# A convolution's prologue reordered: x ahead of the diagonal, its first rows on SP's queue, bands summed on TensorE, exchanged weights on VectorE and GpSimd

## The chip, the cores and the metric

The kernel runs on one core of one Trainium2 chip. The time is the device time of one execution in microseconds; the kernel before took 530.68 us (median of 3 runs, 530.61 to 530.69). The engines are named as in the profile: PE is TensorE (PEld its weight loads), DVE is VectorE, ACT is ScalarE, POOL is GpSimd, SP is SyncE, which here only issues transfers. PSUM is the memory that PE writes; SBUF is the working memory.

## What is computed

A causal convolution with 7 taps along the sequence, one set of taps (a softmax of 7 weights) for each of 8 heads of 24 channels, and behind it a feed-forward network of two products multiplied with each other, and two more products:

```python
w = exp(weight - max); w = w / sum(w)                 # (8 heads, 7 taps)
out[b, s, h, :] = sum_k w[h, k] * x_pad[b, s + k, h, :]   # x_pad: 6 zero rows ahead
x = out.reshape(31232, 192)
a = x @ w1; b = x @ w2                                # 192 -> 1024
h = a * b @ w3                                        # 1024 -> 1024
return h @ w_out                                      # 1024 -> 192
```

x is 8 x 3904 x 192 in float32. The products run in bfloat16; w3 and w_out are multiplied with each other once, so that the last two products become one.

## The kernel before

**Two streams.** The 31232 tokens are cut into two streams (NS = 2, index r) of 15616 tokens, which share every matmul's place on the array: stream r uses rows 64 r to 64 r + 63, where a third of the 192 channels lies (NP = 3 thirds, index k). Tokens are worked in rounds R of 512 per stream (CH). For each round, `first_product` makes 8 feature tiles (index ft) of 128 features: `pa` = x w1 and `pb` = x w2, each of 6 matmuls (3 thirds, 2 streams); ACT copies pa to SBUF (`asb`, line 366) and DVE multiplies it with pb into `abT` (line 367). `second_product` multiplies abT with W_sb = w3 w_out and stores the result.

**Exchanged weights.** Since stream 1 sits on the other 64 rows, half of the weights are needed with their two halves of 64 rows exchanged. `wn[0..2]` hold w1 and w2 as loaded (wn[0] w1's first 128 rows, wn[1] those of w2, wn[2] the last 64 of both); `wsw[0..2]` hold the exchanged copies (`ws` in the profile), which `swap_w(k, lo, hi, engines)` makes for a range of columns with two copies of 64 rows. pa uses wn[0], wsw[0], wn[2] and wsw[2]; pb uses wn[1], wsw[1], wn[2] and wsw[2]. Feature tile ft uses columns 128 ft to 128 ft + 127.

**Convolution.** x is loaded as windows of 32 rows (C), 26 outputs each (ST = C - 6), in batches b of 20 to 80 windows. For each head a band matrix `Aband` of 32x32 carries the taps, so that a window times the band is the convolution (`conv`, line 252, 32x32 places on the array). The band is the same in all four groups of 32 partitions. The result goes by ACT or DVE from PSUM to `convo` (line 260), is transposed (by PE for the first batches, `first_transposes` for batch 0, lines 309 to 321) into `xT`, and feeds `first_product`. `load_x` (lines 105 to 134) issues the transfers of a batch, one for each stream r for batches 0 to 2, all on POOL's queue, with a cast from float32 to bfloat16. The very first window of each stream needs zeros ahead, so it is left out of the runs: DVE zeroes its slot (line 114) and `load_first` (lines 137 to 141) fetches its 26 rows by two more transfers on POOL's queue.

**The bands before.** Line 146 to 150: POOL fills `diag` with ones and selects its diagonal. DVE builds `cmask` for all 7 taps, four copies with a sliding window (lines 162 to 167). The softmax runs on the taps (lines 191 to 199, DVE, ACT, DVE, DVE) into `share`; one matmul (line 201) spreads it over 128 partitions; DVE casts it into `wsb` (line 204), multiplies mask and weights for 8 heads, 7 taps and 32 columns into `cprod` (line 211), and sums the taps by three additions (lines 217 to 220) into Aband.

**What sets the order.** Each engine executes its instructions in the order in which the program lists them (the schedule is manual). POOL's list is: diagonal, batch 0 of x, its first rows, 8 weight transfers in two halves of columns (`load_w`), batches 1 and 2 of x, six exchange copies of the second half of the columns (line 339, 64x512), w_out and four blocks of w3. A transfer on POOL's queue is issued there and its bytes then come in behind those issued before. `warm(n)` puts n matmuls on zeros into PE's list (line 187): 6 at the start, 8 after the spreading, 2 after batch 0's convolution. Four PSUM tiles of two banks ("banks") are used in turn for everything.

The exchange copies of columns 0 to 511 are made by DVE and ACT, the first 256 around `first_transposes` (lines 435 to 437), the second 256 after feature tile 0 (line 459). The convolution of batch 1 follows feature tiles 4 and 5, that of batch 2 feature tile 7 and the next round's 0.

Of the kernel before, what the change touches and what calls it, by code (L numbers as in the profile page):

```python
# [16 lines left out]
def kernel(  # L17
# [84 lines left out]
                runs.append([s, tok(i), 1])  # L102
        return runs

    def load_x(b, parts=(0, 1)):
        tiles = xb_of.setdefault(b, {})
        zeros_of = zero_rows.setdefault(b, [])
        n, m, E = shape_of(b)
        for js in [v for q, v in enumerate(parts_of(b)) if q in parts]:
            xb = work.tile([128, len(js) * m, D], BF16, tag="xb", bufs=6, name="xb")  # L110
            for j in js:
                tiles[j] = (xb, (j - js[0]) * m)
            if b == 0:
                nc.vector.memset(xb[:, 0, :], 0.0)
            for e in range(E):
                for s, t, w in runs_of(b, js, e):
                    for r in range(NS):
                        nc.gpsimd.dma_start(  # L118
                            out=xb[group(r, e), s:s + w, :],
                            in_=bass.AP(tensor=x.tensor, offset=(r * TS + t - PAD) * D,  # L120
                                        ap=[[D, C], [E * ST * D, w], [1, D]]))
# [13 lines left out]


    def load_first():
        xb = xb_of[0][0][0]
        for r in range(NS):
            nc.gpsimd.dma_start(out=xb[Q * r + PAD:Q * r + C, 0, :],  # L140
                                in_=x_rows[r * TS:r * TS + ST, :])
# [6 lines left out]
    nc.gpsimd.affine_select(  # L148
        out=diag, in_=diag, pattern=[[-1, 128 + K - 1]], compare_op=ALU.is_equal,
        fill=0.0, base=0, channel_multiplier=1)  # L150
    ident = diag[:, 0:128]
    zeros = const.tile([128, CH], BF16)
    nc.vector.memset(zeros, 0.0)  # L153
# [6 lines left out]
    one_rows = const.tile([H, 128], BF16)  # L160
    nc.vector.memset(one_rows, 1.0)
    cmask = const.tile([128, K, C], BF16)
    for i in range(4):
        d = diag[i * C:i * C + C, i * C:i * C + C]
        nc.vector.tensor_copy(
            out=cmask[i * C:i * C + C],
            in_=bass.AP(tensor=d.tensor, offset=d.offset, ap=[d.ap[0], [1, K], [1, C]]))
# [16 lines left out]
    def warm(n):  # L184
        t = banks("warm")
        for j in range(n):
# [3 lines left out]

    low = const.tile([H, 1], FP32)
    total = const.tile([H, 1], FP32)
    share = const.tile([H, H, K], BF16)
# [3 lines left out]
    nc.vector.scalar_tensor_tensor(  # L197
        out=share, in0=taps.unsqueeze(1).to_broadcast([H, H, K]), scalar=total,
        in1=diag[0:H, 0:H].unsqueeze(2).to_broadcast([H, H, K]), op0=ALU.mult, op1=ALU.mult)
# [3 lines left out]
    wsb = const.tile([128, H, K, 2], BF16)  # L203
    nc.vector.tensor_copy(
        out=wsb, in_=spread[:, 0, 0:H * K].rearrange("p (h k) -> p h k", h=H)
            .unsqueeze(3).to_broadcast([128, H, K, 2]))
    warm(8)

    Aband = const.tile([128, H, C], BF16)
    cprod = stage.tile([128, H, K, C], BF16, tag="cprod", bufs=1, name="cprod")  # L210
    nc.vector.tensor_tensor(
        out=cprod.rearrange("p h k (s two) -> p h k s two", two=2),
        in0=cmask.rearrange("p k (s two) -> p k s two", two=2).unsqueeze(1)
            .to_broadcast([128, H, K, C // 2, 2]),
        in1=wsb.unsqueeze(3).to_broadcast([128, H, K, C // 2, 2]),
        op=ALU.mult)
    for o, i0, i1 in ((cprod[:, :, 0:3], cprod[:, :, 0:3], cprod[:, :, 4:7]),
                      (cprod[:, :, 0:2], cprod[:, :, 0:2], cprod[:, :, 2:4]),
                      (Aband, cprod[:, :, 0], cprod[:, :, 1])):
        nc.vector.tensor_tensor(out=o, in0=i0, in1=i1, op=ALU.add)  # L220


    xT = [const.tile([128, RING], BF16, name=f"xT{k}", tag=f"xT{k}") for k in range(NP)]
# [85 lines left out]
    def first_transposes(between):  # L309
        n = SIZES[0] // 4  # L310
        convo = convo_of[0]
        for k, f in enumerate((nc.scalar.copy, nc.vector.tensor_copy, nc.vector.tensor_copy)):
            tps = banks_bf16("tps")
            for w in range(n):
                nc.tensor.transpose(  # L315
                    out=tps[:, w, :],
                    in_=convo[:, w, k].rearrange("p r g -> p (r g)"), identity=ident)
            if k == 1:
                between()
            f(out=xT[k][:, 0:4 * n * ST].rearrange("p (c w s) -> p c w s", c=4, w=n),  # L320
              in_=tps[:, 0:n, :].rearrange("p w (c s) -> p c w s", c=4)[:, :, :, 0:ST])

# [75 lines left out]
    def load_wo():  # L398
        nc.gpsimd.dma_start(out=wo_b, in_=wor)
# [51 lines left out]
    def later_loads():  # L451
# [103 lines left out]
```

## Time and profile before

| | us |
|---|---|
| median of 3 runs | 530.68 |
| the profiled execution | 530.6 |
| its span, first to last instruction | 528.9 |
| PE busy | 520.7 (98%) |
| first convolution matmul (line 252) | 7.33 |
| first matmul of the first product (line 360) | 9.90 |
| first multiplication into abT (line 367) | 12.27 |
| convolution of batch 1 | 17.79 |

All times in a view of the profile count from the span's start. The page gives busy times, 40 equal slices of the span, and groups of instructions; the chain of waits goes back from the last instruction to what released it; a timeline lists instructions of an engine in order, merged where the same follow each other (start, length, engine, line, operation, tile, shapes, count, and in brackets the idle time before and what ended it). "Issue" of a transfer is the instruction on the engine whose queue it is; "landing" is when its semaphore is raised.

### The profile page before, as it was taken

The numbers are of one execution on the slowest core, as the hardware profiler recorded it, in microseconds if no ns is written. First come the engines' busy times: TensorE is split into PE (matmuls) and PEld (weight loads), VectorE is DVE, ScalarE is ACT, GpSimd is POOL, SyncE is SP. The second block draws the span as 40 slices with busy tenths as digits, with TensorE's granted clock in tenths as the row PEclk, the third lists the DMA queues.
The fourth block names the chain that finished last, engine by engine and source line by source line (L and its number), as shares of the span: only waits on it lengthen the run. The fifth ranks groups of instructions, "written<-read, shape, count | busy, mean of one in ns | idle before, by whom it ended". The sixth has DMA issues, their size and how long they took to land.

```text
span 528.9 us, 14824 instructions
## 1 busy us (share of the span) xinstructions
PE 520.7 (98%) x6461; PEld 337.8 (64%) x6462; DVE 343.2 (65%) x328; ACT 335.1 (63%) x391; POOL 67.6 (13%) x123
## 2 busy tenths in 40 slices
PE   8999999999999999999999999999999999999997
PEld 3455674856758466584765847558475575856777
DVE  6776549578394774938659295692957839377370
ACT  4867557576574766747667475765757657475562
POOL 9745002004020010301002020020000000000000
PEclk9999999999999999999999999999999999999999
DMA  9999969966699476994769946795317543130304
GB/s 115 182 198 186 141 145 149 148 157 76 145 149 170 97 93 134 128 186 92 106 137 134 178 90 102 143 163 130 56 60 144 101 134 84 62 104 9 113 2 150
DMA packets 135321, 64.69 MB, mean 122 GB/s; under 512 B 88150, under 2 KB 134232, under 8 KB 135256
## 3 DMA queue, kind: packets, MB, share of 16 engines
q1 hardware_dynamic: 92264, 45.63, 41.1%
q0 software_dynamic: 42976, 18.11, 31.8%
q8 instruction: 50, 0.82, 0.6%
q14 instruction: 15, 0.12, 0.1%
q10 hardware_dynamic: 16, 0.00, 0.0%
HBM read 36.22 MB, written 34.80 MB: 134 GB/s over the span
## 4 chain that ended last, share of the span: by engine, by line
PE 94%; DVE 2%; ACT 2%; DMA 1%; issue 1%; POOL 0%; ACTq 0%; POOLq 0%
PE ops L378 31%; PE pa L360 29%; PE pb L360 29%; PE cps L252 3%; DVE abT L367 2%; ACT asb L366 1%; PE wps L418 1%; DMA xb<-in_x_dram 1%; PE w3ps L409 1%; ACT convo L260 0%; POOL xb L118 0%; PE tps L315 0%; DVE xT L307 0%; ACT osb L383 0%; DVE xT L320 0%
## 5 line engine op out<-in xcount | busy, mean ns | idle before, releaser
L367 DVE TENSOR_TENSOR abT<-asb,pb 128x1024 bf16<-128x1024 bf16 (+1 forms) x248 | 298.2, 1204 | 89.9 <-ACT asb L366 72.7
L366 ACT CAST asb<-pa 128x1024 bf16<-128x1024 f32 (+1 forms) x248 | 247.8, 999 | 64.4 <-PE pa L360 63.6
L360 PE MATMUL pb<-xT,wn 64*128 64x512 bf16 (+1 forms) x744 | 199.2, 373 | 0.4
L360 PE MATMUL pa<-xT,wn 64*128 64x512 bf16 (+1 forms) x744 | 198.5, 373 | 0.7 <-DVE xT L307 0.5
L360 PE MATMUL pa<-xT,ws 64*128 64x512 bf16 (+1 forms) x744 | 198.6, 373 | 0.5 <-DVE ws L339 0.4
L360 PE MATMUL pb<-xT,ws 64*128 64x512 bf16 (+1 forms) x744 | 196.5, 373 | 0.0
L360 PEld LDWEIGHTS <-wn 64*128 64x128 bf16 x1488 | 137.3, 94 | 85.1 <-issue 3.5
L360 PEld LDWEIGHTS <-ws 64*128 64x128 bf16 x1488 | 129.8, 94 | 73.2 <-issue 3.4
L378 PE MATMUL ops<-W_sb,abT 128*128 128x192 bf16 x1952 | 168.2, 246 | 0.0
L378 PEld LDWEIGHTS <-abT 128*128 128x128 bf16 x1952 | 159.0, 98 | 9.3 <-issue 9.0
L383 ACT COPY osb<-ops 128x768 f32<-128x768 f32 (+1 forms) x62 | 48.9, 788 | 110.7 <-PE ops L378 110.7
L260 DVE CAST convo<-cps 128x320 bf16<-128x320 f32 (+4 forms) x44 | 31.6, 749 | 76.1 <-PE cps L252 76.1
L118 POOL DMA_DIRECT2D xb<-in_x_dram x74 | 48.4, 663 | 13.0 <-DMA xb<-in_x_dram 5.5
L260 ACT CAST convo<-cps 128x640 bf16<-128x640 f32 (+4 forms) x60 | 34.7, 625 | 5.5 <-PE cps L252 5.3
L510 POOL COPY pace<-abT 1x2 bf16<-1x2 bf16 x9 | 1.6, 174 | 252.9 <-DVE abT L367 252.9
L252 PE MATMUL cps<-xb,Aband 32*32 32x240 bf16 (+2 forms) x1344 | 16.8, 238 | 1.0 <-DMA xb<-in_x_dram 0.8
L252 PEld LDWEIGHTS <-Aband 32*32 32x32 bf16 x1344 | 9.8, 88 | 9.2 <-issue 7.3
L418 PE MATMUL wps<-wo_b,w3T 128*128 128x192 bf16 x64 | 6.6, 246 | 0.2 <-DVE xT L307 0.2
L187 PE MATMUL warm<-zeros 128*128 128x512 bf16 x15 | 5.6, 523 | 1.3 <-DVE zeros L153 1.3
L409 PEld LDWEIGHTS <-w3b 128*128 128x128 bf16 x64 | 3.7, 97 | 3.4 <-issue 3.4
L420 ACT CAST W_sb<-wps 128x192 bf16<-128x192 f32 x8 | 2.5, 318 | 5.1 <-PE wps L418 5.1
L418 PEld LDWEIGHTS <-w3T 128*128 128x128 bf16 x64 | 5.2, 98 | 0.8 <-DVE w3T L412 0.4
(49 smaller groups left out, 51.7 us busy)
## 6 DMA issues: line engine op xcount, KB each, us to landing
out_dram<-osb SPq DMA_DIRECT2D x60, 384.0 KB
xb<-in_x_dram POOLq DMA_DIRECT2D x44, 240.0 KB, 7.7
rows<-convo SPq DMA_DIRECT2D x18, 240.0 KB
rows<-convo SPq DMA_DIRECT2D x18, 150.0 KB
w3b<-in_moe_w_dram POOLq DMA_DIRECT2D x8, 256.0 KB, 9.1
xb<-in_x_dram POOLq DMA_DIRECT2D x6, 228.0 KB, 4.4
xT<-rows SPq DMA_TRANSPOSE x84
rows<-convo SPq DMA_DIRECT2D x11, 120.0 KB
```

Source lines behind the costliest of these rows:

```text
L118: nc.gpsimd.dma_start(out=xb[group(r, e), s:s + w, :], in_=bass.AP(tensor=x.tensor, offset=(r * TS + t - PAD) * D, ap=[[D, C], [E * ST * D ...
L187: nc.tensor.matmul(t[:, j % 2, :], zeros[:, 0:128], zeros, start=True, stop=True)
L252: nc.tensor.matmul(o.rearrange("p (w g) -> p w g", g=wd)[:, :, q * G:(q + 1) * G], Aband[group(r, e), h0 + q, :], xb[group(r, e), s:s + m, ...
L260: f(out=convo[:, e::E, k, :, c0:c0 + c] .rearrange("p w r g -> p r w g"), in_=src[:, :, :, o:o + c])
L360: nc.tensor.matmul(p[:, r, 0:N], w_of(i, k, r)[rs, ft * 128:(ft + 1) * 128], xT[k][rs, r0:r0 + N], start=(k == 0), stop=(k == NP - 1))
L366: nc.scalar.copy(out=asb[:, :, 0:N], in_=pa[:, :, 0:N])
L367: nc.vector.tensor_tensor(out=ab[:, ft, :, 0:N], in0=asb[:, :, 0:N], in1=pb[:, :, 0:N], op=ALU.mult)
L378: nc.tensor.matmul(ops[:, g // 2, (g % 2) * D:(g % 2) * D + D], ab[:, jt, r, g * 128:(g + 1) * 128], W_sb[:, jt, :], start=(jt == 0), stop ...
L383: nc.scalar.copy(out=osb.rearrange("p (a g) d -> p a (g d)", g=2), in_=ops[:, 0:ng // 2, 0:2 * D])
L409: nc.tensor.transpose(out=tps[:, gt, :], in_=w3b[:, gt * 128:(gt + 1) * 128], identity=ident)
L418: nc.tensor.matmul(wps[:, 0, 0:D], w3T[:, gt, :], wo_b[:, gt, :], start=(gt == 0), stop=(gt == JT - 1))
L420: nc.scalar.copy(out=W_sb[:, jt, :], in_=wps[:, 0, 0:D])
```

## The change

It touches only the prologue and the order of the lists.

- **x.** `load_x` takes a list of streams and keeps its tile between calls. Stream 0 of batch 0 is issued as POOL's first instruction, ahead of the diagonal; stream 1 behind the diagonal. The zeroing of the slot and `load_first` go. In their place a float32 tile `begin` is zeroed by DVE, SP's queue fetches the first rows into it, and ACT copies it into the slot.
- **Diagonal.** Its filling with ones moves from POOL to DVE, which waits for nothing; the selection stays on POOL and now waits for DVE.
- **Bands.** The four groups of 32 partitions no longer hold the same: group i gets taps 2i and 2i + 1 (padded from 7 to 8 with a zero in `share`). The mask has 2 taps instead of 7; four small matmuls spread the weights, each to its group; the product is for 2 taps. A matrix `every`, four diagonals side by side in each group (four DVE copies, ahead of the reciprocal in DVE's list), then sums over the groups on PE: four matmuls of 128 columns, two heads' halves times two taps, into one PSUM tile. DVE copies heads 0 to 3 from there, ACT heads 4 to 7. Both read the same PSUM tile, and ACT's copy waits for DVE's. Warm-up matmuls after the spreading are 2, and 4 after the band matmuls, instead of 8.
- **Exchanged weights.** For columns 0 to 255, DVE makes wsw[0] after its convolution copies, POOL wsw[2] and wsw[1] (four 64x256 copies, right after the weight transfers in its list, waiting for wn[2] and wn[1] to land). For 256 to 511, DVE makes wsw[0] and wsw[2] ahead of feature tile 0's multiplication and wsw[1] after it. ACT makes none. `xT2` goes from DVE to ACT.
- **POOL's list** behind that: batch 1 of x, the six second-half copies, batch 2 of x, then w_out and w3. Before, both batches of x came ahead of the copies.

```diff
-    def load_x(b, parts=(0, 1)):
+    def load_x(b, parts=(0, 1), streams=range(NS)):
...
-            xb = work.tile([128, len(js) * m, D], BF16, tag="xb", bufs=6, name="xb")
...
-            if b == 0:
-                nc.vector.memset(xb[:, 0, :], 0.0)
+            if js[0] not in tiles:
+                xb = work.tile([128, len(js) * m, D], BF16, tag="xb", bufs=6, name="xb")
...
-                    for r in range(NS):
+                    for r in streams:
...
-    def load_first():
-        xb = xb_of[0][0][0]
-        for r in range(NS):
-            nc.gpsimd.dma_start(out=xb[Q * r + PAD:Q * r + C, 0, :],
-                                in_=x_rows[r * TS:r * TS + ST, :])
...
-    diag = const.tile([128, 128 + K - 1], BF16)
-    nc.gpsimd.memset(diag, 1.0)
+    load_x(0, streams=(0,))
+
+    zeros = const.tile([128, CH], BF16)
+    nc.vector.memset(zeros, 0.0)
+    diag = const.tile([128, 128 + 8], BF16)
+    nc.vector.memset(diag, 1.0)
     nc.gpsimd.affine_select(
...
-    load_x(0)
-    load_first()
+    begin = stage.tile([128, D], FP32, tag="begin", bufs=1, name="begin")
+    nc.vector.memset(begin, 0.0)
+    for r in range(NS):
+        p = group(r, 0).start
+        nc.sync.dma_start(out=begin[p + PAD:p + C, :], in_=x_rows[r * TS:r * TS + ST, :])
+    load_x(0, streams=(1,))
...
-    cmask = const.tile([128, K, C], BF16)
+    cmask = const.tile([128, 2, C], BF16)
     for i in range(4):
-        d = diag[i * C:i * C + C, i * C:i * C + C]
+        d = diag[i * C:i * C + C, i * C + 2 * i:i * C + 2 * i + C]
...
+    every = const.tile([128, 4, C], BF16)
+    for i in range(4):
+        ps = slice(i * C, i * C + C)
+        nc.vector.tensor_copy(out=every[ps],
+                              in_=diag[ps, ps].unsqueeze(1).to_broadcast([C, 4, C]))
     nc.vector.reciprocal(out=total, in_=total)
...
+    nc.scalar.copy(out=xb_of[0][0][0][:, 0, :], in_=begin)
     spread = banks("spread")
-    nc.tensor.matmul(spread[:, 0, 0:H * K], one_rows, share.rearrange("h a k -> h (a k)"),
-                     start=True, stop=True)
+    for i in range(4):
+        nc.tensor.matmul(
+            spread[i * C:i * C + C, 0, 0:2 * H].rearrange("p (h k) -> p h k", h=H),
+            one_rows, share[:, :, 2 * i:2 * i + 2], start=True, stop=True)
...
-    warm(8)
+    warm(2)
...
-    for o, i0, i1 in ((cprod[:, :, 0:3], cprod[:, :, 0:3], cprod[:, :, 4:7]),
-                      (cprod[:, :, 0:2], cprod[:, :, 0:2], cprod[:, :, 2:4]),
-                      (Aband, cprod[:, :, 0], cprod[:, :, 1])):
-        nc.vector.tensor_tensor(out=o, in0=i0, in1=i1, op=ALU.add)
+    bps = banks("bps")
+    for g in range(2):
+        hs = slice(g * H // 2, (g + 1) * H // 2)
+        for k in range(2):
+            nc.tensor.matmul(
+                bps[:, g, 0:C * H // 2].rearrange("p (h s) -> p h s", s=C),
+                every.rearrange("p i s -> p (i s)"), cprod[:, hs, k, :],
+                start=(k == 0), stop=(k == 1))
+    for g, f in enumerate((nc.vector.tensor_copy, nc.scalar.copy)):
+        f(out=Aband[:, g * H // 2:(g + 1) * H // 2],
+          in_=bps[:, g, 0:C * H // 2].rearrange("p (h s) -> p h s", s=C))
+    warm(4)
...
-        for k, f in enumerate((nc.scalar.copy, nc.vector.tensor_copy, nc.vector.tensor_copy)):
+        for k, f in enumerate((nc.scalar.copy, nc.vector.tensor_copy, nc.scalar.copy)):
...
+    conv(0, 0, 4, evict=(A,))
+    conv(0, 4, 4, evict=(V,))
+    warm(2)
+    swap_w(0, 0, 256, (V, V))
+    for k in (2, 1):
+        swap_w(k, 0, 256, (P, P))
+    first_transposes()
+    for k in (0, 2):
+        swap_w(k, 256, HC, (V, V))
     load_x(1)
-    load_x(2)
     for k in (0, 2, 1):
         swap_w(k, HC, DFF, (P, P))
+    load_x(2)
     load_wo()
     for jt in range(4):
         load_w3(jt)
-    conv(0, 0, 4, evict=(A,))
-    conv(0, 4, 4, evict=(V,))
-    warm(2)
-    first_transposes(lambda: swap_w(0, 0, 256, (V, V)))
-    swap_w(2, 0, 256, (A, A))
-    swap_w(1, 0, 256, (V, A))
...
-        0: seq(*[(swap_w, k, 256, HC, (V, A)) for k in (0, 2, 1)]),
+        0: seq((swap_w, 1, 256, HC, (V, V))),
```

More of the change, by code (lines that the diff above doesn't have):

```diff
@@ L192 @@
     total = const.tile([H, 1], FP32)
[L193 removed]
     nc.vector.reduce_max(out=low, in_=taps, axis=AX.X, negate=True)
     nc.scalar.activation(out=taps, in_=taps, func=ACT.Exp, bias=low, accum_out=total)
+    every = const.tile([128, 4, C], BF16)
[3 more added lines that the diff above has]
+                              in_=diag[ps, ps].unsqueeze(1).to_broadcast([C, 4, C]))
     nc.vector.reciprocal(out=total, in_=total)
     nc.vector.scalar_tensor_tensor(
[L198 removed]
+        out=share[:, :, 0:K], in0=taps.unsqueeze(1).to_broadcast([H, H, K]), scalar=total,
         in1=diag[0:H, 0:H].unsqueeze(2).to_broadcast([H, H, K]), op0=ALU.mult, op1=ALU.mult)
+    nc.scalar.copy(out=xb_of[0][0][0][:, 0, :], in_=begin)
     spread = banks("spread")
[L201 to L210 removed]
+    for i in range(4):
+        nc.tensor.matmul(
+            spread[i * C:i * C + C, 0, 0:2 * H].rearrange("p (h k) -> p h k", h=H),
+            one_rows, share[:, :, 2 * i:2 * i + 2], start=True, stop=True)
+    wsb = const.tile([128, H, 2, 2], BF16)
+    nc.vector.tensor_copy(
+        out=wsb, in_=spread[:, 0, 0:2 * H].rearrange("p (h k) -> p h k", h=H)
+            .unsqueeze(3).to_broadcast([128, H, 2, 2]))
+    warm(2)
+    cprod = stage.tile([128, H, 2, C], BF16, tag="cprod", bufs=1, name="cprod")
     nc.vector.tensor_tensor(
@@ L213 @@
         in0=cmask.rearrange("p k (s two) -> p k s two", two=2).unsqueeze(1)
-            .to_broadcast([128, H, K, C // 2, 2]),
-        in1=wsb.unsqueeze(3).to_broadcast([128, H, K, C // 2, 2]),
+            .to_broadcast([128, H, 2, C // 2, 2]),
+        in1=wsb.unsqueeze(3).to_broadcast([128, H, 2, C // 2, 2]),
         op=ALU.mult)
-    for o, i0, i1 in ((cprod[:, :, 0:3], cprod[:, :, 0:3], cprod[:, :, 4:7]),
-                      (cprod[:, :, 0:2], cprod[:, :, 0:2], cprod[:, :, 2:4]),
-                      (Aband, cprod[:, :, 0], cprod[:, :, 1])):
-        nc.vector.tensor_tensor(out=o, in0=i0, in1=i1, op=ALU.add)
+    Aband = const.tile([128, H, C], BF16)
+    bps = banks("bps")
[10 more added lines that the diff above has]
+    warm(4)
     xT = [const.tile([128, RING], BF16, name=f"xT{k}", tag=f"xT{k}") for k in range(NP)]
@@ L307, in pe_transposes, with first_transposes @@
             (nc.scalar.copy if k == 1 else nc.vector.tensor_copy)(out=dst, in_=src[:, :, :, 0:ST])
[L309 removed]
+    def first_transposes():
         n = SIZES[0] // 4
         convo = convo_of[0]
[L312 removed]
+        for k, f in enumerate((nc.scalar.copy, nc.vector.tensor_copy, nc.scalar.copy)):
             tps = banks_bf16("tps")
```

18 lines of the change are left out of this document (9 added, 9 removed).

## The prediction

> **What bounds the kernel now.** I read the page first: busy times, then the 40 slices.
>
> ```profile
> span 528.9 us, 14824 instructions
> PE 520.7 (98%) x6461; PEld 337.8 (64%) x6462; DVE 343.2 (65%) x328; ACT 335.1 (63%) x391; POOL 67.6 (13%) x123
> PE   8999999999999999999999999999999999999997
> ```
>
> PE is 98% busy and only its first slice shows idleness. Nothing that the change touches lies after the first 20 us, so the question is how much earlier PE gets into its steady work. The chain of waits for the first 20 us, in order of time (start, length, what), shows what holds it there.
>
> ```profile
> 1.50 1.58 POOL xb L118 x2
> 3.09 4.11 DMA xb<-in_x_dram
> ...
> 7.33 0.58 PE cps L252 x32
> ...
> 9.98 0.43 DVE xT L320
> ...
> 11.22 1.02 ACT asb L366
> ...
> 12.27 0.98 DVE abT L367
> ...
> 13.52 0.23 DVE ws L339
> ...
> 13.80 0.61 PE pa L360 x4
> ```
>
> The first convolution (7.33) waits for x; the third feature tile's product (13.80) waits for a DVE exchange copy queued behind abT. The timelines of DVE, POOL and PE's weight loads (start, length, engine, line, idle before) give prices.
>
> ```profile
> 4.52 1.09 DVE L211 TENSOR_TENSOR cprod<-cmask,wsb 128x1792 bf16<-128x1792 bf16 x1
> 5.64 1.02 DVE L220 TENSOR_TENSOR cprod<-cprod 128x768 bf16<-128x768 bf16 x2
> 6.69 0.29 DVE L220 TENSOR_TENSOR Aband<-cprod 128x256 bf16<-128x256 bf16 x1
> ...
> 13.52 0.91 DVE L339 COPY ws<-wn 64x256 bf16<-64x256 bf16 x3
> ```
> ```profile
> 3.09 1.08 POOL L140 DMA_DIRECT2D xb<-in_x_dram  x2
> ...
> 8.86 2.77 POOL L118 DMA_DIRECT2D xb<-in_x_dram  x4
> 11.67 4.02 POOL L339 COPY ws<-wn 64x512 bf16<-64x512 bf16 x6
> ```
> ```profile
> 4.50 0.15 PEld L187 LDWEIGHTS <-zeros 128*128 128x128 bf16 x1 [0.28 <-issue]
> 4.93 0.15 PEld L187 LDWEIGHTS <-zeros 128*128 128x128 bf16 x1 [0.28 <-issue]
> 5.30 0.74 PEld L187 LDWEIGHTS <-zeros 128*128 128x128 bf16 x4 [0.22 <-issue]
> ```
>
> The bands end at 6.98 (6.69 + 0.29), so x and bands bind together: freeing one alone is worth 0.3 us. Warm-up matmuls are 0.42 us apart up to 4.93 and about 0.22 after 5.30. By the groups on each line, times from issue to landing are 4.2 and 4.6 us for x's two streams, 3.8 to 4.1 for its first rows, 4.9 for the first half of w2's 128 rows (wn1; issued 5.72, landed 10.6), and 6.6 and 7.2 for batch 1 of x (issued 8.86 and 9.56, landed 15.5 and 16.7).
>
> **x and its first rows.** Stream 0 is issued at POOL's first free moment, 0.82 instead of 1.50: with 4.2 us it lands at 5.0. Behind it stands the diagonal select (0.29), then stream 1 at 0.82 + 0.91 + 0.29 + gaps = 2.1 instead of 2.40. It lands between 5.0 + 1.3 (the two streams landed 1.3 apart) = 6.3 and 2.1 + 4.6 = 6.7; I take 6.5. The first rows leave POOL (1.08 us less ahead of the weights) for SP's empty queue, behind a zeroing on DVE. Issued near 1.6 and 2.0, they land between 2.0 + 1.7 (the taps on ACT's queue: issued 0.82, not waited for at 2.55) and 2.0 + 4.1 (the same rows on POOL's): 3.7 to 6.1. ACT's copy of them (at most 0.32, the 318 ns of the 128x192 W_sb cast) waits there, and behind it in ACT's queue only work that needs the bands. Cost zero up to 6.1; beyond 6.2 it moves the convolution one for one.
>
> **Bands.** Diagonal and mask start on DVE at 2.1 instead of 1.43, but a mask copy of 64 instead of 224 elements (0.26 each) costs about 0.11, so the maximum over taps still starts near 2.55. New before the reciprocal are four "every" copies of 128 elements: between 0.06 and 0.26 each, I take 0.17, the 224-element row scaled. That is 0.7 from 2.7, and the reciprocal moves from 3.24 to 3.4. The weights' spreading was held by six warm matmuls until 3.95 and now starts there or 0.1 later. Its four matmuls end near 4.4; the cast of 32 elements takes 0.2 (0.27 at 112), the product of 512 elements 0.4 (0.29 at 256, 0.56 at 768): done at 5.0, instead of 5.6 for the product alone. The three additions (1.31) go. In their place: two warm matmuls up to 5.2, four band matmuls (0.1 each) to 5.7, DVE's eviction of half (0.27) to 6.0, ACT's other half only after DVE's, 6.3. Heads 0 to 3 need the first half alone. Four warm matmuls at 0.22 keep PE until 6.5. So bands, PE and x meet at 6.5: first convolution at 6.5 against 7.33, **0.8 earlier**; bounds 0.6 (stream 1 at 6.7) and 1.0 (6.3).
>
> **First transposes and exchange.** xT2 goes from DVE (0.42, third in line at 10.32) to ACT (0.59, right after xT0's 0.59); ACT loses six exchange copies (0.40 each) and DVE has two before xT1 as before. Products that began their last third 3.47 us after the convolution begin it 3.35 after: another 0.1. Then asb 0 (1.01) ends near 11.3 and abT 0 starts at 11.35 instead of 12.27. Four DVE copies (0.23 each, 0.9) moved ahead of abT 0 fit between xT1's end at 9.55 and 11.35; they are hidden by asb 0, and if clashes double them they still are. After abT 0 stand two copies instead of three (0.91, one of them 0.636 beside a POOL copy): 0.46 undisturbed, 0.9 with a clash; I take 0.7. So abT 1 starts 11.35 + 1.22 + 0.7 = 13.3 against 14.46: **1.15 earlier**, bounds 0.95 and 1.4. The wait for ws at 13.80 becomes a wait for abT.
>
> **POOL's queue.** This is where the gain can go back. POOL now copies 0:256 of ws2 and ws1 ahead of batch 1. No row has a 64x256 POOL copy: half of the 64x512 (0.30) below; 0.17 (the 1x2 copy's row) plus half of the rest, 0.39, above. I take 0.35, with gaps 0.75 for ws1's two. They wait for wn1. Its issue moves from 5.72 to 4.4 (first rows gone, x earlier), so with 4.9 us it lands at 9.3; if the stream of transfers is the limit it moves only as far as x does, 0.75, to 9.85. I take 9.6. Then ws1 is done at 10.35, just when PE ends pa 0 (10.3): no stall. Behind: two issues of batch 1 (1.38; 10.35 to 11.75), six second-half copies (4.02) to 15.8, then batch 2, wo_b and w3, all issued 1 to 6 us later than before. Feature tile 4 needs the last copy for its pb: 15.9 against 17.05, again **1.15 earlier**. Batch 1 is needed after tile 4, at 16.65 (17.79 - 1.15). Batch 2 was landed by 19.3 and is needed near 22.7; w3's first block landed at 22.6 and is needed at 27.2: later issues are covered by 3 to 4 us.
>
> **Sum.** From tile 4 on, order and work are the old ones, so 1.15 stays to the end. The profiled execution took 530.6 (span 528.9 and 1.7 around it), 0.08 below the median of 530.68. 530.6 - 1.15 = 529.45, rounded to 529.5. Terms together give 529.1 to 530.0 for this case. About 0.2% (1.06 us) is what a measurement of this kernel can tell from no change; the forecast lies just beyond it.
>
> At the clash of DVE and POOL copies the row is 636 ns for one DVE copy against a median of 222. The Trainium skill, SBUF — State Buffer, Who interferes with whom, says that the port pair shared by VectorE's two-port copies and GpSimd is an exclusive lock held for the whole instruction; the row agrees. By that rule every DVE copy beside POOL's could wait for a whole POOL copy, and with all of them the estimate would be about 0.4 us less gain, by the row only one in three did.
>
> **Rivals.**
> (a) POOL's chain eats most of it. If wn1 lands where it did, at 10.6, or its copies wait for DVE's, the last second-half copy ends at 10.6 + 0.05 + 0.75 + 1.38 + 4.02 = 16.8 and tile 4 gains only 0.2. For it: wn1's 4.9 us were over 1 us more than the other weights of that half (3.3 to 3.8), so it may again be the late one. Against it: x's stream ends earlier. With half of that, 530.1.
> (b) Slower: batch 1 comes late. It is issued at 10.35 and 11.05 instead of 8.86 and 9.56. If its transfers keep 6.6 and 7.2 us from issue to landing, the second lands at 18.25, and the convolution after tile 4, at 17.79 before, starts at 18.4; with wn1 at 10.6 it is 19.4, 1.6 late: 530.6 + 1.6 = 532.2. It decides from a landing at 17.7 on, one for one. Against it: these 7.2 us were mostly queueing behind weights that will have drained.
> (c) Clock. Warm-up work is interrupted more (two small groups inside). If the half pace seen before 5.30 lasts until the first products, four warm matmuls cost 0.8 more and convolution and transposes about 0.8: 529.5 + 1.6 = 531.1. The Trainium skill, TensorE: Matmul & The Clock Gate, What's actually happening, has PE at half clock until a window of about 3.4 us was busy; the pace doubling 4 us after the first matmul at 1.27 agrees with it. By that rule the new pauses of some 0.3 us should not matter.
> (d) x does not land earlier because the transfers' start is not bound to the issue: then the convolution starts at 7.2, and only the exchange's 0.4 remains: 530.2.
>
> **Numbers.** Forecast 0.62, 0.09 of it at a gain under 1.06; (a) 0.10; (b) 0.14, at its full price; (c) 0.08, half of it with more matmuls at half pace, beyond 531.7; (d) 0.06. Faster by over 0.2%: 0.62 - 0.09 = 0.53. Slower by over 0.2%: 0.14 + 0.04 = 0.18. Within: 0.29. The range runs from 528.9 (abT 1 at 1.4 earlier, some later PE gaps shrinking too) to (b)'s 532.2; the likeliest case's own is 529.1 to 530.0.
>
> **What would show it.** First convolution near 6.5 with x's stream 1 as its last wait; no addition on DVE; no wait for ws at tile 2; POOL's copies of ws1 ending near 10.4 and its second-half copies near 15.8; the convolution of batch 1 near 16.7. Wrong would be: wn1 landing after 10.2, batch 1 landing after 16.7, warm matmuls still 0.42 apart at 6, or the first rows on SP's queue landing after 6.2.

## The result and the profile after

The changed kernel is slower: 532.11 us (median of 14 executions, 531.05 to 532.97) against 530.71 us (14 executions, 530.51 to 531.29), a ratio of 1.0023 with a 95% interval of 1.0015 to 1.0031. That is 1.4 us more where 1.15 less was forecast. The profiled execution took 531.84.

First the page of the kernel after: its span, PE's busy share and PE's 40 slices.

```profile
span 530.1 us, 14840 instructions
PE 521.5 (98%) x6466; PEld 338.1 (64%) x6467; DVE 343.4 (65%) x333; ACT 334.7 (63%) x388; POOL 68.0 (13%) x124
PE   7999999999999999999999999999999999999997
```

Only the first slice differs from before (7 instead of 8), and the span is 1.2 us longer: again everything happens in the first 20 us. The chain of waits there, in order of time (start, length, what):

```profile
1.40 0.87 POOL xb L118
...
2.35 0.34 POOL diag L145
...
2.71 0.17 DVE cmask L167
...
3.76 0.15 DVE low L195
...
4.93 0.28 DVE share L203
...
5.25 0.20 PE spread L209 x3
5.45 0.97 PE warm L189 x2
6.42 0.43 PE bps L230 x4
6.84 1.61 PE warm L189 x4
8.45 0.72 PE cps L269 x64
...
13.30 0.92 DVE abT L382
```

Before, this chain began with the wait for x. Now it runs from x's first issue through the diagonal, the mask, the softmax and the warm-up matmuls to the first convolution at 8.4, which was at 7.33 before and forecast at 6.5. From there the distances are those of before: first multiplication into abT at 13.30 (12.27 before), the second at 15.56 (14.46), the convolution of batch 1 at 18.93 (17.79). So the loss of 1.0 to 1.2 us is complete at the first convolution, and nothing behind it gains.

The timeline of POOL after (start, length, engine, line, operation, shapes, count, idle before):

```profile
1.40 0.87 POOL L118 DMA_DIRECT2D xb<-in_x_dram  x1 [0.87 <-POOLq L557]
2.35 0.33 POOL L145 TENSOR_SCALAR_AFFINE_SELECT diag<-diag 128x136 bf16<-128x136 bf16 x1
2.60 0.74 POOL L118 DMA_DIRECT2D xb<-in_x_dram  x1
```

POOL stands idle for 0.87 us ahead of the first transfer: being first in its list brought stream 0 of x from 1.50 to 1.40, not to 0.82. The diagonal's selection, which stood at 1.10 before, is now at 2.35. That is the trade: x 0.1 us earlier, the diagonal 1.25 us later. What it feeds is on DVE's timeline:

```profile
2.71 1.02 DVE L167 COPY cmask<-diag 32x64 bf16<-32x64 bf16 x4 [1.06 <-POOL diag L145]
3.76 0.15 DVE L195 TENSOR_REDUCE low<-taps 8x1 f32<-8x7 f32 x1
```

DVE waits 1.06 us for the diagonal, and the maximum over the taps, which needs no diagonal, stands in the queue behind the mask. PE's timeline and its weight loads show the price:

```profile
5.25 0.20 PE L209 MATMUL spread<-share,one_rows 8*32 8x16 bf16 x4 [1.24 <-DVE share L203]
...
6.64 1.82 PE L189 MATMUL warm<-zeros 128*128 128x512 bf16 x4
```
```profile
7.07 0.15 PEld L189 LDWEIGHTS <-zeros 128*128 128x128 bf16 x1 [0.28 <-issue]
7.49 0.15 PEld L189 LDWEIGHTS <-zeros 128*128 128x128 bf16 x1 [0.28 <-issue]
```

PE pauses for 1.24 us, and the warm-up matmuls are still 0.42 apart at 7.07 and 7.49, the pace that had doubled by 5.3 before. The granted clock in the windows view is 1.00 in every stretch of the first 14 us, before and after, so this pace has to be read from the spacing. The four warm matmuls fill 6.84 to 8.45; two conditions of the convolution end just ahead of them: x's stream 1 (issued 2.60, 5.6 us to landing: 8.2) and the bands (7.2 for heads 0 to 3, ACT's half near 7.5). At full pace the convolution would have waited for x until 8.2 all the same. That nearness matters below.

Stream 1 was late because the transfers themselves slowed down. The windows view (stretch, its length, busy time of each engine with instructions in brackets, granted clock, busy share of the transfer engines, summed over packets that can overlap, GB/s), first after, then before:

```profile
5.00:6.00 1.00, 0.75 (x6) 0.38 (x6) 0.67 (x3) 0.30 (x1) 1.00 (x3) 1.00 1.28 141
6.00:7.00 1.00, 1.00 (x6) 0.58 (x5) 0.27 (x2) 0.00 (x0) 1.00 (x3) 1.00 1.12 141
```
```profile
5.00:6.00 1.00, 1.00 (x6) 0.42 (x5) 0.97 (x2) 0.00 (x0) 1.00 (x3) 1.00 1.60 190
6.00:7.00 1.00, 0.55 (x3) 0.05 (x1) 0.92 (x3) 0.00 (x0) 0.90 (x2) 1.00 1.43 190
```

For two microseconds the transfers moved 141 GB/s where they moved 190 before, a quarter less. No view shows why.

### The profile page after: what moved, and what is told of

It reads as the page before. It is cut to its first block, busy times and chain, and to the rows that moved or that the text cites. A ratio compares the mean times of both kernels' runs of the same rounds, so it can differ in the third digit from the quotient of the medians.

```text
span 530.1 us, 14840 instructions
## 1 busy us (share of the span) xinstructions
PE 521.5 (98%) x6466; PEld 338.1 (64%) x6467; DVE 343.4 (65%) x333; ACT 334.7 (63%) x388; POOL 68.0 (13%) x124
## 4 chain that ended last, share of the span: by engine, by line
PE 94%; DVE 3%; ACT 2%; issue 1%; POOL 0%; POOLq 0%; ACTq 0%
PE ops L393 31%; PE pa L375 29%; PE pb L375 29%; PE cps L269 3%; DVE abT L382 2%; ACT asb L381 1%; PE wps L433 1%; PE w3ps L424 1%; PE warm L189 0%; ACT convo L277 0%; DVE ws L354 0%; DVE convo L277 0%; DVE cmask L167 0%; POOL xb L118 0%; DVE every L200 0%
## 5 line engine op out<-in xcount | busy, mean ns | idle before, releaser
L269 PE MATMUL cps<-xb,Aband 32*32 32x240 bf16 (+2 forms) x1344 | 16.8, 238 | 0.2 <-DVE abT L382 0.2
```

Of the source, the lines that this page charges most:

```text
L269: nc.tensor.matmul(o.rearrange("p (w g) -> p w g", g=wd)[:, :, q * G:(q + 1) * G], Aband[group(r, e), h0 + q, :], xb[group(r, e), s:s + m, ...
```

## Experiments

The theory that the profile after suggests: the diagonal behind x comes 1.25 us late, so the spreading does, so PE pauses and keeps its half pace, and this holds the convolution. Its rivals: the transfers of x themselves are late; or the exchange or the bands bring the loss. Medians and ratios are against the kernel before, run on the same chip beside each (530.78 to 530.87); places in time come from one profiled execution each, so a place can differ in the other executions.

**The three parts, each alone on the kernel before.** First the load part with the diagonal's move:

```diff
+    load_x(0, streams=(0,))
+    zeros = const.tile([128, CH], BF16)
+    nc.vector.memset(zeros, 0.0)
...
-    nc.gpsimd.memset(diag, 1.0)
+    nc.vector.memset(diag, 1.0)
...
-    load_x(0)
-    load_first()
+    begin = stage.tile([128, D], FP32, tag="begin", bufs=1, name="begin")
+    nc.vector.memset(begin, 0.0)
+    for r in range(NS):
+        p = group(r, 0).start
+        nc.sync.dma_start(out=begin[p + PAD:p + C, :], in_=x_rows[r * TS:r * TS + ST, :])
+    load_x(0, streams=(1,))
...
+    nc.scalar.copy(out=xb_of[0][0][0][:, 0, :], in_=begin)
```

> The kernel before with the load part alone: stream 0 of x ahead of the diagonal, diagonal's ones by DVE, first rows by SP's queue and ACT; bands and exchanged weights as before. Theory D (the diagonal): POOL's first transfer starts at 1.40 whatever stands ahead of it (it did in the changed kernel, though POOL was free at 0.82), so x gains 0.1 us and the selection, with it mask, taps and bands, comes 1.25 late: bands at about 8.2 instead of 7.0, time 531.7 to 532.2. Theory X (the transfers): it is stream 1 that comes late (8.2 instead of 7.0), because of SP's rows or the order, and the convolution starts at 8.3 for that reason; time again about 531.8, but then the last wait before the convolution is x and its landing, not the bands, is the later of the two. If the load part is harmless: 530.5 to 530.9.

532.15 us, ratio 1.0023 (1.0013 to 1.0032): the whole loss, with the old bands and the old exchange. Its chain:

```profile
2.34 0.34 POOL diag L146
...
4.93 0.20 PE spread L202
5.13 3.52 PE warm L187 x8
8.66 0.98 PE cps L253 x41
```

x's stream 1 landed at 7.0 here and the bands were done at 7.95; eight warm matmuls at half pace (3.52 us) hold the convolution at 8.6. Late x is not needed for the loss. (The profiled execution is the slowest of its ten, 532.90; its places behind the convolution are not typical.) The pace is what held last, but not the only thing that came late: at full pace the bands would still have held the convolution until 7.95, 0.6 later than before.

Next the bands alone (mask of two taps, four spreading matmuls, `every`, band matmuls, two and four warm matmuls; loads and exchange as before):

```diff
-    warm(8)
+    warm(2)
...
-        nc.vector.tensor_tensor(out=o, in0=i0, in1=i1, op=ALU.add)
...
+            nc.tensor.matmul(
+                bps[:, g, 0:C * H // 2].rearrange("p (h s) -> p h s", s=C),
+                every.rearrange("p i s -> p (i s)"), cprod[:, hs, k, :],
+                start=(k == 0), stop=(k == 1))
...
+    warm(4)
```

> The kernel before with the band part alone: two taps for each group of partitions, sum over groups on TensorE, warm-up of 2 and 4 matmuls; loads and exchanged weights as before. Theory D: the diagonal is early again, so the bands are done near 6 and PE's clock has risen by 5.3; the convolution waits for x alone, 7.2 instead of 7.33: 530.4 to 530.7. Theory C (the clock): the pauses inside the new chain alone keep PE at half pace until about 8, four warm matmuls take 1.6 us and the convolution starts near 7.7 to 8.4: 531.2 to 532.

530.99 us, 1.0002 (0.9993 to 1.0011): neutral, and between the two expected ranges. The first half of the bands was done at 6.0 instead of 6.98, but the convolution began at 7.26, because x and its first rows came at 6.9 to 7.3 as before (and the warm matmuls, at half pace until 6.7 though PE had hardly paused (0.07 us), ended at 7.16).

And the exchange alone:

```diff
+    swap_w(0, 0, 256, (V, V))
+    for k in (2, 1):
+        swap_w(k, 0, 256, (P, P))
+    first_transposes()
+    for k in (0, 2):
+        swap_w(k, 256, HC, (V, V))
     load_x(1)
-    load_x(2)
...
-        0: seq(*[(swap_w, k, 256, HC, (V, A)) for k in (0, 2, 1)]),
+        0: seq((swap_w, 1, 256, HC, (V, V))),
```

> The kernel before with the exchange part alone: ws2 and ws1 of columns 0 to 255 on POOL, the next 256 columns on DVE, xT2 on ACT, batch 2 of x behind POOL's copies. By the prediction's working 0.3 to 0.5 us faster (530.2 to 530.4). By the trace of the changed kernel, where abT 1 kept the same distance from the convolution (7.18 us against 7.13 before) since a DVE copy beside POOL's took 654 ns: nothing, 530.6 to 530.9. If POOL's queue becomes the limit: 531 to 531.5.

531.28 us, 1.0010 (1.0001 to 1.0018): it costs 0.5 us by the medians instead of gaining. DVE's timeline and PE's:

```profile
13.54 1.12 DVE L337 COPY ws<-wn 64x256 bf16<-64x256 bf16 x2
14.70 2.35 DVE L365 TENSOR_TENSOR abT<-asb,pb 128x1024 bf16<-128x1024 bf16 x2
```
```profile
14.72 0.39 PE L358 MATMUL pb<-xT,ws 64*128 64x512 bf16 x2 [0.64 <-DVE ws L337]
```

The two last copies take 0.45 and 0.67 us beside POOL's 64x512 copies, where 0.22 is a copy's undisturbed length, and pb of tile 2 waits 0.64 for them. The second abT begins at 14.70, 0.24 later than before, and batch 1's convolution at 18.06, 0.27 later. The time is in the range expected for POOL's queue as the limit, but the wait in the trace is for DVE's copies.

**Undoing the one step.** The changed kernel, with the diagonal filled and selected on POOL ahead of x, as before; all else stays.

```diff
-    load_x(0, streams=(0,))
...
-    nc.vector.memset(diag, 1.0)
+    nc.gpsimd.memset(diag, 1.0)
     nc.gpsimd.affine_select(
...
+    load_x(0, streams=(0,))
```

> The changed kernel with one thing undone: the diagonal's ones and selection stand on POOL ahead of x again. Theory D: the first transfer starts at 1.50 instead of 1.40, the selection ends at 1.4 instead of 2.68, the bands are done at 6.0 or earlier, PE has no pause of 1.2 us and reaches full clock at 5.3: the convolution starts at 7.0 to 7.3, limited by x; time 530.2 to 530.7. Theory X: stream 1 still lands at about 8.2 and the convolution starts at 8.3: 531.6 to 532.1.

530.79 us, 0.9997 (0.9988 to 1.0006): the whole loss is gone, with the first rows still on SP's queue. Its chain:

```profile
1.10 0.29 POOL diag L143
...
2.40 4.56 DMA xb<-in_x_dram
...
7.01 0.77 PE cps L268 x63
...
12.04 0.92 DVE abT L381
```

The spreading starts at 4.08 with next to no pause (0.06 us), the four warm matmuls end at 6.75, and the convolution waits for x (landed 6.97). It is 0.3 earlier than before, and the exchange gives that back: the second abT at 14.28 against 14.46, the convolution of batch 1 at 17.64 against 17.79.

**Which of the two behind the step: the queue on DVE or x?** Now x stays first, but DVE's list has the maximum ahead of the mask and the `every` copies behind the softmax's end.

```diff
+    nc.vector.reduce_max(out=low, in_=taps, axis=AX.X, negate=True)
     cmask = const.tile([128, 2, C], BF16)
...
-    nc.vector.reduce_max(out=low, in_=taps, axis=AX.X, negate=True)
     nc.scalar.activation(out=taps, in_=taps, func=ACT.Exp, bias=low, accum_out=total)
-    every = const.tile([128, 4, C], BF16)
...
     nc.vector.reciprocal(out=total, in_=total)
...
             one_rows, share[:, :, 2 * i:2 * i + 2], start=True, stop=True)
+    every = const.tile([128, 4, C], BF16)
...
     wsb = const.tile([128, H, 2, 2], BF16)
```

> The changed kernel with DVE's list alone altered: the maximum over the taps ahead of the mask copies, the four copies of the diagonal for the sum over groups behind the weights' share. The diagonal is as late as in the changed kernel (2.7). Theory D+Q (the late diagonal hurts because the softmax stands behind the mask in DVE's queue, and the pause of PE then costs the clock): taps are ready at 2.5, the spreading starts near 4.1 instead of 5.25, PE pauses 0.1 us, the bands are done 0.5 to 0.7 earlier and the convolution starts at 7.0 to 7.6: 530.7 to 531.3. Theory that the late diagonal itself is the cause, queue or not: 531.6 or more.

532.57 us, 1.0033 (1.0022 to 1.0045). DVE and PE did what was expected and the time did not. PE's timeline:

```profile
4.25 0.19 PE L204 MATMUL spread<-share,one_rows 8*32 8x16 bf16 x4 [0.23 <-DVE share L198]
4.37 0.60 PE L192 MATMUL warm<-zeros 128*128 128x512 bf16 x2
...
5.99 1.03 PE L192 MATMUL warm<-zeros 128*128 128x512 bf16 x4
6.95 0.22 PE L269 MATMUL cps<-xb,Aband 32*32 32x120 bf16 x1
8.46 0.73 PE L269 MATMUL cps<-xb,Aband 32*32 32x120 bf16 x63 [1.28 <-DMA xb<-in_x_dram]
```

The pause is 0.23 us, two warm matmuls take 0.60 (full pace) already at 4.4, and the convolution's first matmul is there at 6.95. Then PE waits 1.28 us for stream 1 of x, which took 5.8 us to land, against 4.6 before. So a second hold stands behind the first: with x first, x itself came later in this execution.

**The pace alone.** Three more warm matmuls bridge the pause; nothing is moved.

```diff
-    warm(6)
+    warm(9)
```

> The changed kernel with 9 instead of 6 warm-up matmuls at the start, so that PE has work through its pause of 1.24 us (4.0 to 5.25); nothing else. Theory C (the pause costs the clock, and the four warm matmuls ahead of the convolution at half pace hold it): full clock is reached near 5 instead of 8.2, the four take 0.9 instead of 1.6 us, the convolution starts at 7.5 instead of 8.4: 530.9 to 531.3. Theory that late bands or x hold the convolution: no change, 531.8 to 532.3.

532.01 us, 1.0018 (1.0009 to 1.0027). PE's timeline:

```profile
5.24 0.19 PE L209 MATMUL spread<-share,one_rows 8*32 8x16 bf16 x4
...
6.40 1.03 PE L189 MATMUL warm<-zeros 128*128 128x512 bf16 x4
7.35 0.74 PE L269 MATMUL cps<-xb,Aband 32*32 32x120 bf16 x64
```

The spreading is as late as in the changed kernel (5.24), yet the convolution is 1.0 us earlier (7.35): the pace did hold it. But x was in time in this execution, too: stream 1 landed at 7.2, and with a landing at 8.2, as in the changed kernel, the convolution could have gained 0.2 at most. The gain is then lost, by its own chain:

```profile
4.45 5.89 DMA wn<-in_moe_w_dram
...
11.82 0.41 POOL ws L354
...
13.21 1.22 DVE abT L382
```

The first w1 block landed at 9.6, wn[2] 5.9 us after its issue at 10.3, and the first abT begins at 13.21, where the changed kernel had it at 13.30. POOL's four copies wait for these weights, and pb of tile 0 waits 0.5 us for POOL's copies: a dependence that the exchange part added. The eleven executions fall into two groups: three took 531.05 to 531.14, inside the expected 530.9 to 531.3, and eight, the profiled one among them, 531.91 to 532.36. It may be that the transfers lag in the eight and not in the three; there is no profile of the three, so this is not shown.

**No warm matmuls behind the bands.**

```diff
-    warm(4)
```

> The changed kernel without the four warm-up matmuls between the sum over groups and the convolution. Theory C: the convolution starts when the bands are there, at 7.2 to 7.3, instead of 8.4; but the clock stays low longer, which the first products pay back in part: 531 to 531.7. If x's stream 1 really lands at 8.2 there each time, the convolution starts at 8.3 and nothing is gained: 531.8 to 532.5.

532.99 us, 1.0039 (1.0026 to 1.0052). The convolution starts at 7.22, but PE stays at half pace, and convolution, transposes and first product all pay:

```profile
7.22 1.00 PE cps L268 x54
...
9.18 1.60 PE tps L331 x15
10.78 1.41 PE pa L374 x6
```

In the changed kernel's chain the convolution takes 0.72, and its transposes end 1.28 after they began; here that is 1.81 by PE's timeline. Matmuls of the first product are 0.43 apart up to 12.4 and 0.21 from 12.7. What is gained at the convolution, 1.2 us, is gone at the first abT (13.26 against 13.30), and the two exchange copies behind it take 1.33 us instead of 0.98.

**What makes x late?** Three runs on the lag. First, the rows on POOL's queue again instead of SP's, on max_first:

```diff
-    begin = stage.tile([128, D], FP32, tag="begin", bufs=1, name="begin")
...
-        nc.sync.dma_start(out=begin[p + PAD:p + C, :], in_=x_rows[r * TS:r * TS + ST, :])
     load_x(0, streams=(1,))
+    load_first()
```

> The kernel with the maximum first (bands done at 6.5, so that x alone holds the convolution) with one more thing undone: x's first rows come by two transfers on POOL's queue behind both streams again, none on SP's. There stream 1 landed at 8.4, 2.8 after stream 0, because one of 16 engines sent its last packets of x until 8.1. Theory S (the rows on SP's queue, whose packets ran at 4 among x's, put an engine behind): the lag goes from x, rows land at 7.2 to 7.5, convolution at 7.5: 530.9 to 531.4. Theory G (the order of the transfers on POOL: a selection between the streams): lag and time stay, 532 to 532.7.

532.10 us, 1.0028 (1.0017 to 1.0039). Stream 1 landed at 7.9, the rows at 8.1 and 8.3, the convolution started at 8.25. Stream 1 took 5.4 us here, so the lag does not need SP's two transfers.

Second, both streams ahead of the selection, on max_first:

```diff
-    load_x(0, streams=(0,))
+    load_x(0)
...
-    load_x(0, streams=(1,))
```

> The kernel with the maximum first, with both streams of x issued ahead of the selection of the diagonal, instead of one ahead and one behind; rows on SP's queue. The selection comes 0.7 later (ends near 3.4), so the bands are done near 7.0 to 7.2. Theory G (the gap between the streams): stream 1 lands at 6.9 without lag and the convolution starts near 7.3: 530.9 to 531.4. Theory S: lag of 1.2 us on x or on the first weights as before, 532 to 532.7.

533.12 us, 1.0043 (1.003 to 1.0055), the slowest of all. Stream 1, issued at 2.23, landed at 6.9, and w1's first block 4.6 us after its issue, as with the diagonal first (4.5): no lag. But the selection is at 3.04 and the chain is that of the changed kernel, later still (convolution at 8.6):

```profile
3.04 0.34 POOL diag L145
...
7.09 1.59 PE warm L191 x4
```

So a late selection holds the convolution also where no transfer lags. This kernel loses more behind that. DVE's timeline:

```profile
11.82 2.21 DVE L353 COPY ws<-wn 64x256 bf16<-64x256 bf16 x4
14.06 1.22 DVE L381 TENSOR_TENSOR abT<-asb,pb 128x1024 bf16<-128x1024 bf16 x1
```

POOL, early here, made its 64x512 copies beside DVE's four, which took 2.21 us (1.27 in the changed kernel), and the first abT waited for them until 14.06. The prediction had these four hidden by asb 0 even with clashes.

Third, a selection without use between the two streams, on diag_first, which opens the gap of the changed kernel with the diagonal first:

```diff
     load_x(0, streams=(0,))
+    spare = const.tile([128, 128 + 8], BF16)
+    nc.gpsimd.affine_select(
+        out=spare, in_=diag, pattern=[[-1, 128 + 8]], compare_op=ALU.is_equal,
+        fill=0.0, base=0, channel_multiplier=1)
```

> The kernel with the diagonal first (530.79, stream 1 landed at 6.97) with a second, unused selection of the same size on POOL between the two streams of x, so that stream 1 is issued near 2.7 to 2.8 instead of 2.40. Theory G: x or the first weights come with a lag of 1.2 us and the time goes to 531.6 to 532.3. Theory S or chance: stream 1 lands 0 to 0.3 later, 530.7 to 531.2.

531.16 us, 1.0009 (1.0000 to 1.0018). In the profiled execution (530.82) stream 1, issued at 2.72, took 4.6 us and landed at 7.28: no lag, against what a gap as its whole cause asks for. But the eleven executions lie between 530.63 and 532.17, four of them above 531.9, while those of diag_first lie between 530.4 and 531.03. The gap may bring the lag in some executions; one profile can't tell.

**The exchange, with the diagonal first.** Before's exchange on diag_first, and then the change's exchange with the last two copies on ACT instead of DVE:

```diff
...
     first_product(0, {
-        0: seq((swap_w, 1, 256, HC, (V, V))),
+        0: seq(*[(swap_w, k, 256, HC, (V, A)) for k in (0, 2, 1)]),
```

> The changed kernel with the diagonal on POOL ahead of x again and with the exchanged weights as in the kernel before (ACT and DVE, both batches of x ahead of POOL's copies). The exchange part cost 0.3 us from the convolution on in its own trace (abT 1 at 14.70 against 14.46, with a DVE copy of 0.67 beside POOL's), and the diagonal first lets the convolution start at 7.0. Theory: both add up, 530.3 to 530.5, faster than the kernel before. If ACT's and DVE's old copies eat the earlier start: 530.6 to 530.8.

530.32 us, 0.9995 (0.9986 to 1.0004).

```diff
-        0: seq((swap_w, 1, 256, HC, (V, V))),
+        0: seq((swap_w, 1, 256, HC, (A, A))),
```

> The kernel with the diagonal first, with the two exchange copies behind feature tile 0's multiplication (ws1, columns 256 to 511) on ACT instead of DVE. They took DVE 0.96 us there, 0.67 of it one copy beside POOL's; pb of tile 2 waited 0.56 for them. Theory (the clash on DVE costs the exchange part its gain): abT 1 starts at about 13.9 instead of 14.28, tile 2 no longer waits for DVE's copy, time 530.3 to 530.5. If ACT, whose asb 1 is then 0.8 later, is the next limit: 530.7 to 530.9.

530.42 us, 0.9993 (0.9984 to 1.0002). ACT's timeline:

```profile
11.94 0.82 ACT L353 COPY ws<-wn 64x256 bf16<-64x256 bf16 x2
```

Two copies take 0.82 there, right behind the first asb, and no wait of pb for ws is left at tile 2; the second abT begins at 13.82 (14.28 with the copies on DVE), the convolution of batch 1 at 17.15 (17.64). The two copies in DVE's list are what cost the exchange its gain. How much of it is their clash with POOL's copies is not separated: undisturbed they would take 0.46 there, they took 0.96, and with both gone asb 1 on ACT, not DVE, holds the second abT. Both kernels are 0.45 us below the kernel before by their medians, but both intervals reach past 1: whether they beat it isn't settled.

## Why the prediction was wrong, step by step

- **"Stream 0 is issued at POOL's first free moment, 0.82."** This is the first step that failed. POOL's first transfer began at 1.38 to 1.40 in all seven kernels that have x first, with POOL free from 0.70; with the diagonal ahead it begins at 1.50. Moving x ahead was worth 0.1 us, not 0.68, and the selection behind it stood at 2.35, not near 1.75. That the order of these two at the head of POOL's list costs the loss is shown both ways: the load part alone brings all of it (loads_only), and the diagonal moved back alone takes all of it away (diag_first). How the loss divides between PE's pace and late transfers is not shown: with the pause nearly gone or bridged (max_first, warm_bridge) the medians stayed at 532.57 and 532.01.
- **"Diagonal and mask start on DVE at 2.1 ... so the maximum over taps still starts near 2.55."** The mask started at 2.71, and a copy of 64 elements took 0.17 (one of them 0.46), not the 0.11 scaled from 224 elements; the four took 1.02, the old ones 1.09. The maximum started at 3.76 and the spreading at 5.25, forecast at 3.95 or 0.1 later. The prediction had the maximum queued behind the mask, and let a saved 0.6 us that didn't exist make up for the later diagonal. Undoing the step (diag_first) brought the maximum back to 2.42 and the loss to nothing.
- **"Four warm matmuls at 0.22 keep PE until 6.5."** They ran at twice that, 1.61 us in all. Rival (c) named it and gave it 8 in 100, but with the small pauses inside the new chain as its cause. Those are not it: bands_only has that chain with an early diagonal and lost nothing. The cause was the 1.24 us of the late spreading. In the four kernels where PE paused 0.8 us or more ahead of the spreading (changed kernel, loads_only, no_warm4, max_first_x_together), the half pace lasted to 7.9 or longer; in the ten with a pause of 0.23 us or none it had ended by 6.8, each in one execution. Bridged, the convolution came 1.0 us earlier, with x in time too. The Trainium skill, TensorE: Matmul & The Clock Gate, What's actually happening, says that the window of about 3.4 us is free-running and that its phase differs from run to run. The runs agree that the moment varies: without a long pause the pace doubled anywhere from 4.4 or a little before (max_first, exchange_only) to 6.7 (bands_only). The shortest stretch, 3.1 us from PE's first matmul at 1.27 to full pace at 4.37 in max_first, is a little under the 3.4 of the Trainium skill. The prediction's reading of that rule, that pauses of some 0.3 us should not matter, held for the 0.23 us of max_first. In no_warm4 a second pause, 0.38 us at 6.84, was followed by half pace until 12.4 to 12.7; one execution cannot tell whether that pause or the phase of the window did this. No run shows the window's borders.
- **x at 6.5.** It landed at 8.2, only 0.2 of it by a later issue than before: stream 1 took 5.6 us, 5.8 in max_first and 4.6 before, and the transfers moved 141 GB/s from 5 to 7 instead of 190. In loads_only, no_warm4 and warm_bridge stream 1 was in time (7.0 to 7.2), and w1's first block lagged: 4.9, 5.2 and 6.3 us from issue to landing against 4.5 in diag_first. So all six kernels with x first and the selection between its streams show a lag in the one place or the other (max_first_rows_pool in stream 1, 5.4), small in loads_only, and the one with both streams together shows none. The rows on SP's queue are neither needed for it (max_first_rows_pool) nor enough (diag_first). The gap between the streams remains the suspect, but with the diagonal first its profile showed no lag, and no run shows a mechanism: this stays open.
- **Bands, from the spreading on.** Sized well: the product 0.42 (0.4), the eviction 0.29 (0.27). Their worth was not: with x at 7.0 to 7.3 nothing is gained by bands at 6.0 (bands_only).
- **Exchange.** "I take 0.7" for the two copies behind abT 0: 0.98, with 0.67 for one beside POOL. The bound with a clash was 0.9. The "another 0.1" up to the first abT: it came 4.92 us after the convolution, 4.94 before. From the first convolution to the second abT it is 7.18 us after and 7.13 before: the 0.35 of gain did not come. The Trainium skill, SBUF — State Buffer, Who interferes with whom, has the shared port pair as an exclusive lock for a whole instruction; 0.67 against 0.22 undisturbed fits it, and so does diag_first_act, where ACT's two copies beside POOL's took 0.40 each, as ACT's copies did before.
- **POOL's queue.** The prices were right: 64x256 copies 0.39 each (0.35 taken), six second-half copies 3.94 (4.02). Rival (a)'s end of POOL's chain came true without deciding anything: wn1 landed at 10.20 (9.6 taken), and the last second-half copy ended at 16.80, (a)'s 16.8 and not the 15.8 of the forecast. Tile 4's pb, which needs it, came at 18.13, because everything ahead of it was late; at the 15.9 of the forecast it would have waited 0.9 for that copy. Rival (b) did not occur: batch 1 was issued at 11.41 and 12.13, its second stream landed at 16.8, and its convolution at 18.93 did not wait for it.
- **First rows on SP's queue.** Harmless, as costed: ACT's copy of them ran at 4.95 and took 0.35 us (at most 0.32 taken).

The sum was a gain of 0.8 at the convolution and 0.35 behind it, up to the second abT. In its place stand losses of 1.05 and 0.05, and 0.1 more up to the end of the span. Of the prediction's signs of being wrong, warm matmuls still 0.42 apart at 6 was plain; wn1 (landed 10.20, sign from 10.2) and batch 1 (16.8, sign from 16.7) stood on the line.

## What to carry to other kernels

Before moving a transfer to the head of a queue, look at what that head can do: here 0.1 us was to be had, and the small instruction that was pushed back fed a chain on DVE, ACT and PE. Here a pause in the warm-up cost PE's pace for microseconds after it, so the late small chain could be paid twice: the first convolution stood at 7.0 with the diagonal first, at 7.35 with the chain late and the pause bridged, and at 8.4 with the pause and late x. Where several conditions end within a few tenths (here pace, x and bands), removing one shows the next; here only undoing the common origin gave the time back.

## What was not expected of the hardware

- The first transfer on POOL's queue began no earlier than 1.38 to 1.40 us into the span, in seven kernels, with the engine free from 0.70; what it waited for is not shown.
- DVE copies over 32 partitions cost about the same for 64 elements (0.17 to 0.18 us), 128 elements (0.17 to 0.19) and little more for 224 (0.26 to 0.27). In the groups of 64 and 128 elements one or two of four took 0.26 to 0.46. Of these 25 long ones in eleven kernels, 24 ended within 0.03 us of the end of a transfer's issue on POOL (in the changed kernel at 3.35, with the issue of stream 1 ending at 3.34). They seem to wait for the end of that issue; the copies of 224 elements beside the same issues do not, and no run tests it.
- PE's half pace lasted to anywhere between 4.4 us (max_first) and 12.7 us (no_warm4), and to between 4.4 and 6.7 among kernels without a long pause, with the granted clock of those stretches at 1.00.
- The same 228 KB transfer, stream 1 of batch 0, took 4.4 to 5.8 us to land among kernels that issue it between 2.2 and 2.7; which one it would be, no view of the profile told ahead.
